# One scan-and-convolution kernel: B times x over the whole array, B turned on TensorE, and a new order of all operations

## The chip, the cores and the metric

The kernel runs on one core of a Trainium2 chip. Its time is device microseconds of one execution; several are taken and the median counts. A profile of one more execution, with its own time and span, tells what each engine did.

## What is computed

Two sequence mixers over S = 2048 positions and D = 640 channels, side by side in one output of 1280 columns. Part A is a diagonal complex state space with 640 states; part B is a four-tap convolution, a gate, and a convolution as long as the sequence.

```python
# part A                                     # part B
B_bar = ((Lam_bar - 1) / Lam)[:, None] * B   k_shift = sum_j k[t - j] * shift_k[:, j]      # 4 taps
Bu    = einsum("bld,pd->blp", x, B_bar)      kv      = k_shift * v
h_t   = Lam_bar * h_{t-1} + Bu_t             y       = causal_conv(kv, ssm_k) + kv * ssm_D # by FFT
y     = 2 * Re(h @ C^T) + x * Dskip          out_B   = q * y
```

## The kernel before, in words

All of it lives in one SBUF tile, `arena`, and one PSUM tile, `acc`, of eight banks of 512 columns. A state's real part stands in partitions 0 to 63 and its imaginary part in 64 to 127, 64 states to a block, ten blocks `j`.

Part A. `load_B` (L482) brings B's real and imaginary rows: the first 256 as plain rows, which TensorE turns against an identity (`turn_B`, L501) and `ev_B` (L503) empties from PSUM, the last 384 by two DMA transposes (L489). `load_x` (L519) brings x by eight DMA transposes, `ld_x0` to `ld_x7`, 256 positions each. `up2`, `up1` and `up0` (L564, L582, L601) form B times x, accumulating over five slices of the 640 channels (`base`, L555), and gather pairs, fours and eights of positions with small rotations `RR` (`rmm`, L577); `ev_up...` empties each result into the tile `A`. A block `up2` is 20 matmuls of up to 512 columns in two banks. Then a scan over coarse positions (`coarse`, `cs_...`), the way back down (`down`: `dn`, and the additions `ad`), and the product with C (`project`: `C`, `ev_C`, with x times Dskip, `xd`, added).

Part B. Four taps (`cm`, products, L198 and L199; `ca`, sums, L799; `cx`, the gate, L800) make kv, which goes to DRAM (`pl`) and comes back in another layout (`rl`). The long convolution is a transform in two steps (`s1`, emptied by `e1`, L845; `s2`, emptied by `e2`, L872) of the filter h and of kv, their product (`pp`, `pq`, `py`, `pz`, L883 to L890), and the way back (`r2`, `r1`). `s1h` needs h, with `ssm_D` added by `addD0` (L768) on GpSimd, and a table `f1` (L274).

The tables are made on the chip, of whole numbers and a sine: GpSimd makes phases (`w_q` L291, `g_q` L330, `phs` L449, `phc` L452, each over 1024 or 1280 columns of int32), ScalarE takes their sine (`w_s`, `g_s`, `sin`, `cos`). The parameters of part A go through a chain of small operations, on VectorE up to `fi` (L378), on GpSimd from `fn1` (L386) to `ph` (L390), on ScalarE `al_s` (L394), on VectorE `al` (L396); four instructions `rr` (L436, 128 x 1280) spread the result to `RR`, which `up1` and `up0` multiply by.

The order is written out by hand: `ORDER` (L1060) lists every operation by number, with its engine (T TensorE, V VectorE, A ScalarE, G GpSimd, S the SyncE queue) and the first of its PSUM banks. Each engine works through its own operations in that order. `emit` (L122) adds the waits: for what an operation reads or overwrites, and, at the first operation of a group, for the last user of its banks. An operation that waits holds up everything behind it on its engine. `warm` (L505) are matmuls of zeros.

What the change and the steps below touch: `load_B`, `BT` (L469), `base`, `rmm` and `ORDER`. In them, `base` issues for each slice d two matmuls of 64 columns, one to each half of the array:

```python
for d in range(5):
    for r in range(2):
        e.matmul(o[64 * r:64 * r + 64], lhsT=self.BT[j][:, r, d, :], rhs=self.XP[:, d, lo:lo + n], start=(d == 0),
                 stop=(d == 4), skip_group_check=True, tile_position=(0, 64 * r))
```

Of the kernel before, what the change touches and what calls it, by code (L numbers as in the profile page):

```python
# [12 lines left out]
bf16 = mybir.dt.bfloat16  # L13
# [447 lines left out]
def mmc(n, par=1):  # L461
    return n * 0.000422 / par


class PartA:
    def __init__(self, c):
        self.c = c
        v = c.v
        self.A = v("A").rearrange("p (j g x) -> p j g x", j=10, g=8)  # L469
        self.BT = []  # L470
        for n, lo in ((2, 0), (2, 1280), (6, 2560)):
            blk = v("BT", lo, 640 * n).rearrange("p (r d j m) -> p r d j m", r=2, d=5, j=n)
            self.BT += [blk[:, :, :, j] for j in range(n)]
# [8 lines left out]
    def load_B(self, k):  # L482
        c, P = self.c, self.c.P
        srcs = ((0, c.ins["A_B_re"]), (1, c.ins["A_B_im"]))
        if k == 2:
            for ri, src in srcs:
                dst = c.v("BT", 2560 + 1920 * ri, 1920).rearrange("p (d m) -> p d m", d=5)
                s = src[256:640, :].rearrange("p (d q) -> p d q", q=128)
                P.add(f"ld_B{k}", {PSP: 1.4}, lambda e, dst=dst, s=s: e.dma_start_transpose(out=dst, in_=s), outs=[dst], nbytes=384 * 1280)  # L489
            return  # L490
        raw, idn = c.v("T", 1280 + 1280 * k, 1280), c.I3[:, 0:128]
# [4 lines left out]
        for r in range(2):  # L496
            g, out, part = P.group(1), c.v("BT", 1280 * k + 640 * r, 640), raw[:, 640 * r:640 * r + 640]
# [5 lines left out]
            P.add("ev_B", {PDVE: .5, PACT: .7}, lambda e, B, out=out: c.CP[e](out=out, in_=B.bitcast(bf16)[:, 0:640]), outs=[out], group=g)  # L503
# [51 lines left out]
    def base(self, e, o, j, lo, n):  # L555
        for d in range(5):
            for r in range(2):
                e.matmul(o[64 * r:64 * r + 64], lhsT=self.BT[j][:, r, d, :], rhs=self.XP[:, d, lo:lo + n], start=(d == 0),  # L558
                         stop=(d == 4), skip_group_check=True, tile_position=(0, 64 * r))
# [4 lines left out]
    def up2(self, j0, q, parts):  # L564
# [3 lines left out]
        for lo, n in parts:  # L568
# [3 lines left out]
            P.add(f"up2{q}_{j0}", {PPE: 10 * .108 * n}, mm, ins=self.base_in(j0, 4 + 2 * q + lo, n) + [self.BT[j0 + 1]], group=g, nmm=20)  # L572
# [4 lines left out]
    def rmm(self, e, o, n, j, x):  # L577
        for r in range(2):
            e.matmul(o[64 * r:64 * r + 64], lhsT=self.c.RR[:, n, j, 64 * r:64 * r + 64], rhs=x, start=False,
                     stop=True, skip_group_check=True, tile_position=(0, 64 * r))  # L580

    def up1(self, j0):  # L582
# [13 lines left out]
        P.add(f"up1_{j0}", {PPE: 12 * .216}, mm, ins=ins, group=g, nmm=24)  # L596
# [359 lines left out]
def build(c):  # L956
# [9 lines left out]
    for k in range(3):  # L966
        a.load_B(k)
# [202 lines left out]
```

## Time and profile before

| what | value |
|---|---|
| median of 3 runs | 198.95 us (196.23 to 199.26) |
| the profiled execution | 199.76 us, span 197.9 us |
| busy: TensorE, VectorE, ScalarE, GpSimd | 178.1, 173.3, 134.0, 76.5 us |
| mean granted TensorE clock | 0.975 |
| moved by DMA | 30.19 MB, 153 GB/s |
| base matmuls of 64 columns (L558) | 440, busy 46.8 us |

The span runs from the first to the last instruction of the profiled execution. Rows of the order of time read: start, length, engine, line, operation, what is written and read, count, and in brackets the idle time before it with what ended it. A matmul's own length holds its fill and its wait in the pipeline, so the pace of matmuls is read from the length of a group on the chain, not from one of them.

### The profile page before, as it was taken

The numbers are of one execution on the slowest core, as the hardware profiler recorded it, in microseconds if no ns is written. First come the engines' busy times: TensorE is split into PE (matmuls) and PEld (weight loads), VectorE is DVE, ScalarE is ACT, GpSimd is POOL, SyncE is SP. The second block draws the span as 40 slices with busy tenths as digits, with TensorE's granted clock in tenths as the row PEclk, the third lists the DMA queues.
The fourth block names the chain that finished last, engine by engine and source line by source line (L and its number), as shares of the span: only waits on it lengthen the run. The fifth ranks groups of instructions, "written<-read, shape, count | busy, mean of one in ns | idle before, by whom it ended". The sixth has DMA issues, their size and how long they took to land.

```text
span 197.9 us, 7928 instructions
## 1 busy us (share of the span) xinstructions
PE 178.1 (90%) x3546; PEld 119.9 (61%) x3549; DVE 173.3 (88%) x230; ACT 134.0 (68%) x160; POOL 76.5 (39%) x63
## 2 busy tenths in 40 slices
PE   5699999779999999788978999999999999999970
PEld 1386555345567765556656666567677867887750
DVE  3969998999789899999999999999999999858650
ACT  2076999845998798999969799796377640870000
POOL 6869972940020400341704465840220604605000
PEclk9799999969999999999999999999999999999996
DMA  6999999599599999899993899002599805433995
GB/s 140 224 206 160 170 170 146 125 183 176 121 231 213 174 179 124 134 193 137 149 251 80 223 165 192 8 3 68 114 211 213 168 14 155 111 85 83 233 208 160
DMA packets 106685, 30.19 MB, mean 153 GB/s; under 512 B 101275, under 2 KB 106011, under 8 KB 106651
## 3 DMA queue, kind: packets, MB, share of 16 engines
q1 hardware_dynamic: 106158, 29.18, 81.0%
q8 instruction: 28, 0.46, 1.1%
q10 hardware_dynamic: 492, 0.50, 1.0%
q14 instruction: 7, 0.05, 0.1%
HBM read 11.32 MB, written 7.86 MB: 97 GB/s over the span
## 4 chain that ended last, share of the span: by engine, by line
PE 41%; DVE 20%; POOL 16%; DMA 9%; issue 7%; ACT 5%; DVEq 0%; ACTq 0%; POOLq 0%
PE acc L718 17%; PE acc L558 8%; POOL arena L291 5%; POOL arena L799 4%; PE acc L904 4%; ACT arena L872 4%; PE acc L859 3%; DMA arena<-in_B_ssm_D_dram 3%; PE acc L840 3%; POOL arena L330 3%; PE acc L925 2%; DMA kv_rows<-arena 2%; DMA arena<-in_A_Lambda_re_dram 2%; DVE arena L872 2%; DVE arena L198 2%
## 5 line engine op out<-in xcount | busy, mean ns | idle before, releaser
L558 PE MATMUL acc<-arena 128*64 128x512 bf16 (+1 forms) x440 | 46.8, 369 | 0.1
L718 PE MATMUL acc<-arena 128*128 128x320 bf16 x320 | 45.7, 300 | 0.6 <-DVE arena L720 0.4
L872 ACT CAST arena<-acc 128x960 bf16<-128x960 f32 (+1 forms) x38 | 33.3, 910 | 9.2 <-PE acc L859 7.4
L718 PEld LDWEIGHTS <-arena 128*128 128x128 bf16 x320 | 30.4, 98 | 13.3 <-DVE arena L720 1.0
L558 PEld LDWEIGHTS <-arena 128*64 128x64 bf16 x440 | 24.6, 113 | 18.7 <-issue 2.4
L845 ACT CAST arena<-acc 128x1024 bf16<-128x1024 f32 x32 | 31.1, 1024 | 7.0 <-PE acc L840 6.6
L909 ACT CAST arena<-acc 128x1024 bf16<-128x1024 f32 x18 | 17.4, 1026 | 9.9 <-PE acc L904 9.8
L859 PE MATMUL acc<-arena 128*64 128x160 bf16 x512 | 21.8, 235 | 1.4 <-ACT arena L845 0.4
L859 PEld LDWEIGHTS <-arena 128*64 128x64 bf16 x512 | 18.1, 110 | 6.4 <-ACT arena L872 1.7
L710 POOL TENSOR_TENSOR arena<-arena 128x640 bf16<-128x640 bf16 x9 | 12.3, 1399 | 15.9 <-DVE arena L888 9.3
L799 DVE TENSOR_TENSOR arena<-arena 128x2048 bf16<-128x2048 bf16 x13 | 18.2, 1401 | 0.3
L720 DVE TENSOR_TENSOR arena<-acc,arena 128x640 bf16<-128x640 f32 x16 | 13.1, 823 | 5.8 <-PE acc L718 4.8
L799 POOL TENSOR_TENSOR arena<-arena 128x2048 bf16<-128x2048 bf16 x2 | 8.3, 4154 | 22.5 <-DVE arena L198 22.5
L886 POOL TENSOR_TENSOR arena<-arena 128x1280 bf16<-128x1280 bf16 x4 | 10.6, 2656 | 16.2 <-DVE arena L883 10.7
L701 DVE TENSOR_TENSOR arena<-acc,arena 128x1024 bf16<-128x1024 f32 (+1 forms) x14 | 16.1, 1169 | 0.3 <-PE acc L682 0.2
L888 POOL TENSOR_TENSOR arena<-arena 128x1280 bf16<-128x1280 bf16 x3 | 8.3, 2772 | 20.0 <-DVE arena L886 19.9
L840 PE MATMUL acc<-arena 64*64 64x64 bf16 x960 | 11.8, 195 | 4.4 <-POOL arena L330 2.5
L840 PEld LDWEIGHTS <-arena 64*64 64x64 bf16 x960 | 9.6, 108 | 9.9 <-issue 4.1
L937 DVE TENSOR_TENSOR arena<-acc,arena 128x960 bf16<-128x960 f32 (+1 forms) x12 | 12.1, 1041 | 2.1 <-PE acc L925 2.1
L198 DVE TENSOR_SCALAR arena<-arena 128x2048 bf16<-128x2048 bf16 (+2 forms) x19 | 12.6, 674 | 1.1 <-issue 0.5
L682 PE MATMUL acc<-arena 128*128 128x512 bf16 (+2 forms) x50 | 12.3, 328 | 0.5 <-ACT arena L845 0.5
L883 DVE TENSOR_TENSOR arena<-arena 128x2560 bf16<-128x2560 bf16 x8 | 12.0, 1504 | 0.2
(142 smaller groups left out, 289.3 us busy)
## 6 DMA issues: line engine op xcount, KB each, us to landing
out_dram<-arena SPq DMA_DIRECT2D x32, 160.0 KB, 3.5
arena<-in_B_ssm_k_dram SPq DMA_DIRECT2D x8, 320.0 KB, 6.4
kv_rows<-arena SPq DMA_DIRECT2D x5, 512.0 KB, 3.5
arena<-kv_rows SPq DMA_DIRECT2D x16, 160.0 KB, 4.4
arena<-in_A_x_dram SPq DMA_DIRECT2D x16, 160.0 KB, 3.6
arena<-in_B_q_dram SPq DMA_DIRECT2D x8, 320.0 KB, 5.7
arena<-in_A_B_im_dram ACTq DMA_DIRECT2D x2, 160.0 KB, 4.1
arena<-in_A_B_re_dram ACTq DMA_DIRECT2D x1, 160.0 KB
```

Source lines behind the costliest of these rows:

```text
L198: vm = lambda e: lambda out, in_, by: e.tensor_scalar_mul(out=out, in0=in_, scalar1=by)
L558: e.matmul(o[64 * r:64 * r + 64], lhsT=self.BT[j][:, r, d, :], rhs=self.XP[:, d, lo:lo + n], start=(d == 0), stop=(d == 4), skip_group_che ...
L682: e.matmul(B[:, o], lhsT=c.RR[:, n, j, :], rhs=fr(j, q, k), start=not by_pe, stop=True, skip_group_check=True)
L701: e.tensor_tensor(out=o, in0=b, in1=o, op=ALU.add)
L718: e.matmul(B[:, 512 * b:512 * b + 320], lhsT=lh[j], rhs=self.CT[:, j, 320 * b:320 * b + 320], start=(j == 0), stop=(j == 9))
L720: P.add(f"ev_C{i}", {PDVE: dve(640)}, lambda e, B: e.tensor_tensor(out=ys.rearrange("p (b n) -> p b n", b=2), in0=B.rearrange("p (b n) -> ...
L799: P.add(f"ca{d}_{j}", tt, lambda e: e.tensor_tensor(out=t1, in0=t1, in1=t2, op=ALU.add), outs=[t1], ins=[t1, t2])
L840: e.matmul(B[64 * b:64 * b + 64, 512 * l + 64 * i:512 * l + 64 * i + 64], lhsT=lh[i][ps], rhs=F[ps, b, 64 * l:64 * l + 64], start=True, st ...
L845: P.add(f"e1{what}{hf}_{u}", {PACT: act(1024), PDVE: dve(1024)}, lambda e, B: c.CP[e](out=out, in_=(B.rearrange("p (l n s k) -> p k s l n" ...
L859: e.matmul(B[64 * s:64 * s + 64, 512 * b + 160 * i:512 * b + 160 * i + 160], lhsT=c.W[:, k, 64 * b:64 * b + 64], rhs=self.AS[hf][:, k, 160 ...
L872: c.CP[e](out=out, in_=b.rearrange("p r (k j n) -> p r k j n", k=n, j=4) if nj > 1 else b.rearrange("p r (k x) -> p r k x", k=n))
L909: P.add(f"er2{hf}_{u}", {PACT: act(1024), PDVE: dve(1024)}, lambda e, B: c.CP[e](out=out, in_=B.rearrange("p (s n b) -> p b s n", s=2, n=4 ...
```

## The change

`base` and `rmm` issue one matmul of 128 columns in place of two of 64, so the weights of a block stand together: `BT` is laid out by 128 rows, five equal pieces, instead of three pieces of different shape. All 640 rows of B now come as plain rows, ten loads of 160 KB, and TensorE turns each (ten `turn_B`, ten `ev_B`, where there were four); the two DMA transposes of B are gone. `ORDER` is new from end to end.

```diff
-        if k == 2:
-            for ri, src in srcs:
-                dst = c.v("BT", 2560 + 1920 * ri, 1920).rearrange("p (d m) -> p d m", d=5)
-                s = src[256:640, :].rearrange("p (d q) -> p d q", q=128)
-                P.add(f"ld_B{k}", {PSP: 1.4}, lambda e, dst=dst, s=s: e.dma_start_transpose(out=dst, in_=s), outs=[dst], nbytes=384 * 1280)
-            return
-        raw, idn = c.v("T", 1280 + 1280 * k, 1280), c.I3[:, 0:128]
+        raw, idn = c.v("T", 1280 + 1280 * k, 1280) if k < 2 else c.v("Y", 1280 * k, 1280), c.I3[:, 0:128]
...
-            g, out, part = P.group(1), c.v("BT", 1280 * k + 640 * r, 640), raw[:, 640 * r:640 * r + 640]
+            g, part = P.group(1), raw[:, 640 * r:640 * r + 640]
+            out = c.v("BT", 1280 * k, 1280).rearrange("p (d j r m) -> p d j r m", d=5, j=2, r=2)[:, :, :, r]
...
     def base(self, e, o, j, lo, n):
         for d in range(5):
-            for r in range(2):
-                e.matmul(o[64 * r:64 * r + 64], lhsT=self.BT[j][:, r, d, :], rhs=self.XP[:, d, lo:lo + n], start=(d == 0),
-                         stop=(d == 4), skip_group_check=True, tile_position=(0, 64 * r))
+            e.matmul(o, lhsT=self.BT[j][:, d, :], rhs=self.XP[:, d, lo:lo + n], start=(d == 0), stop=(d == 4), skip_group_check=True)
...
     def rmm(self, e, o, n, j, x):
-        for r in range(2):
-            e.matmul(o[64 * r:64 * r + 64], lhsT=self.c.RR[:, n, j, 64 * r:64 * r + 64], rhs=x, start=False,
-                     stop=True, skip_group_check=True, tile_position=(0, 64 * r))
+        e.matmul(o, lhsT=self.c.RR[:, n, j, :], rhs=x, start=False, stop=True, skip_group_check=True)
...
-    for k in range(3):
+    for k in range(5):
         a.load_B(k)
...
 ORDER = (
-    "152A0 50G0 140S0 109V0 0V0 75V0 145G0 98G0 6T0 26G0 141G0 153A0 77S0 38G0 146S0 147A0 41G0 168S0 78A0 22G0 13G0 8G0 14V0 "
+    "159A0 41G0 0V0 75V0 6T0 76S0 153A0 8G0 77S0 26G0 13G0 134G0 78A0 15V0 100G0 170S0 50G0 2T1 19V0 7G0 33V0 164A0 16V0 135G0 "
...
```

Lines behind `load_B` shift by five to nine in the changed file: L575 becomes L568, L599 L590, L799 L790, L840 L831, L558 L552.

First place: the SyncE queue at the start, with the semaphores that each transfer waits for (there are eight, taken in turn, so a transfer waits until the one eight before it has landed). Before:

```order
L749 DMA arena<-in_B_shift_k_dram 128x5x4
L348 DMA arena<-in_A_Lambda_im_dram 10x2x64 [waits DVE_49]
L494 DMA arena<-in_A_B_re_dram 128x640
L524 DMA_TRANSPOSE arena<-in_A_x_dram 128x5x256
L489 DMA_TRANSPOSE arena<-in_A_B_im_dram 128x5x384 [waits DMAHW1_49]
L524 DMA_TRANSPOSE arena<-in_A_x_dram 128x5x256 [waits DMAHW2_49]
L489 DMA_TRANSPOSE arena<-in_A_B_re_dram 128x5x384 [waits DMAHW3_49]
L773 DMA_TRANSPOSE arena<-in_B_k_dram 128x2048 [waits DMAHW4_49]
L524 DMA_TRANSPOSE arena<-in_A_x_dram 128x5x256 [waits DMAHW5_49]
```

Now (`ld_x7` is the first of L519, `ld_x6` the second, `ld_x4` the third; five more loads of B stand on ScalarE's queue):

```order
L348 DMA arena<-in_A_Lambda_re_dram 10x2x64 [waits DVE_49]
L348 DMA arena<-in_A_Lambda_im_dram 10x2x64
L488 DMA arena<-in_A_B_re_dram 128x640
L488 DMA arena<-in_A_B_im_dram 128x640
L488 DMA arena<-in_A_B_re_dram 128x640 [waits DMAHW1_49]
L488 DMA arena<-in_A_B_im_dram 128x640 [waits DMAHW3_49]
L519 DMA_TRANSPOSE arena<-in_A_x_dram 128x5x256 [waits DMAHW4_49]
L519 DMA_TRANSPOSE arena<-in_A_x_dram 128x5x256 [waits DMAHW5_49]
L488 DMA arena<-in_A_B_im_dram 128x640 [waits DMAHW6_49]
L519 DMA_TRANSPOSE arena<-in_A_x_dram 128x5x256 [waits DMAHW7_49]
L740 DMA arena<-in_B_shift_k_dram 128x5x4 [waits DMAHW0_49]
L519 DMA_TRANSPOSE arena<-in_A_x_dram 128x5x256 [waits DMAHW1_49]
```

The first x stood behind one load of B on this queue and now stands behind four; k has moved behind x5 and the first piece of h.

Second place: VectorE ahead of the eviction of `up1_0` (L599, now L590). Before, from `ca0_1` to `ca0_0`; `al` (L396) and two `rr` stand further up, ahead of `ev_up20_2`:

```order
L799 TENSOR_TENSOR arena<-arena 128x2048
L416 TENSOR_TENSOR arena<-arena 128x20 [waits DVE_49]
L436 TENSOR_TENSOR arena<-arena 128x1280
L198 TENSOR_SCALAR arena<-arena 128x2048 [waits DVE_49]
L436 TENSOR_TENSOR arena<-arena 128x1280
L575 CAST arena<-acc 128x2x2x256 [waits PE_49,Activation_49]
L599 CAST arena<-acc 128x2x2x256 [waits PE_49]
L799 TENSOR_TENSOR arena<-arena 128x2048 [waits DVE_49]
```

Now, from `al`, right behind `ev_up20_0`, to `ca0_1`; `ev_up1_0` (L590) and `ev_up20_2` (L568) are the next two:

```order
L396 TENSOR_TENSOR arena<-arena 128x80 [waits Activation_49]
L436 TENSOR_TENSOR arena<-arena 128x1280 [waits DVE_49]
L402 MEMSET arena 64x1
L436 TENSOR_TENSOR arena<-arena 128x1280
L274 TENSOR_TENSOR arena<-arena 128x256 [waits Activation_49]
L402 MEMSET arena 64x1
L436 TENSOR_TENSOR arena<-arena 128x1280
L790 TENSOR_TENSOR arena<-arena 128x2048 [waits DMAHW2_49,Activation_49]
L568 CAST arena<-acc 128x2x2x256 [waits PE_49]
L198 TENSOR_SCALAR arena<-arena 128x2048 [waits DMAHW3_49,DVE_49,Pool_49]
L402 MEMSET arena 64x1
L790 TENSOR_TENSOR arena<-arena 128x2048 [waits DVE_49]
```

`al` has moved behind the eviction of `up20_0`, three `rr` follow it at once, and the fourth has gone to GpSimd, behind `addD0`.

Third place: TensorE ahead of the first `s1h` (L840, now L831). Before, behind `up1_4`:

```order
L579 LDWEIGHTS arena
L579 MATMUL acc<-arena 64x512
L840 LDWEIGHTS arena [waits DMAHW1_49,DMAHW3_49,DMAHW0_49,DMAHW4_49,DVE_49,Pool_49]
L840 MATMUL acc<-arena 64x64
L840 LDWEIGHTS arena
```

Now, behind `up21_8`:

```order
L552 LDWEIGHTS arena
L552 MATMUL acc<-arena 128x512
L511 LDWEIGHTS arena [waits DVE_49]
L511 MATMUL acc<-arena 128x512
L511 LDWEIGHTS arena
L511 MATMUL acc<-arena 128x512
L831 LDWEIGHTS arena [waits DMAHW2_49,DMAHW0_49,DMAHW6_49,DVE_49,Pool_49]
L831 MATMUL acc<-arena 64x64
```

`up1_4` has moved behind the first three `s1h`, and `warm0` (L511) stands ahead of them. `warm0` and `s1h0_9` use the bank of `up1_0`, `s1h0_1` that of `up20_2`; VectorE empties both.

More of the change, by code (lines that the diff above doesn't have):

```diff
@@ L595, in up1 @@
             ins += self.base_in(j, 2, 2) + [self.A[:, j, 4:6, 0:256], c.RR[:, 0, j, :]]
[L596 removed]
+        P.add(f"up1_{j0}", {PPE: 12 * .216}, mm, ins=ins, group=g, nmm=12)
         out = self.A[:, j0:j0 + 2, 2:4, 0:256]
@@ L965, in build @@
     b.load_small()
-    for k in range(3):
+    for k in range(5):
         a.load_B(k)
```

11 lines of the change are left out of this document (5 added, 6 removed), and 75 rows, old and new, of the table ORDER.

## Prediction

> **What bounds the kernel now.** I read the page's first part, then the stretches of ten microseconds, then the order of time on each engine up to 45 us, because the new table moves most there.
>
> ```profile
> span 197.9 us, 7928 instructions
> PE 178.1 (90%) x3546; PEld 119.9 (61%) x3549; DVE 173.3 (88%) x230; ACT 134.0 (68%) x160; POOL 76.5 (39%) x63
> PEclk9799999969999999999999999999999999999996
> GB/s 140 224 206 160 170 170 146 125 183 176 121 231 213 174 179 124 134 193 137 149 251 80 223 165 192 8 3 68 114 211 213 168 14 155 111 85 83 233 208 160
> ```
> Two engines are nearly full, TensorE and VectorE. The stretches (busy time of PE, PEld, DVE, ACT, POOL, then clock, DMA share, GB/s) show where each has room:
>
> ```profile
> 20.00:30.00 10.00, 10.00 (x96) 5.29 (x94) 9.72 (x5) 9.82 (x10) 8.56 (x6) 1.00 1.42 170
> 30.00:40.00 10.00, 8.27 (x78) 4.11 (x74) 9.68 (x12) 9.07 (x9) 6.42 (x3) 1.00 0.86 137
> 40.00:50.00 10.00, 9.22 (x214) 4.99 (x216) 9.82 (x12) 5.59 (x5) 2.02 (x2) 0.83 0.89 171
> 60.00:80.00 20.00, 19.24 (x341) 13.83 (x340) 18.92 (x27) 16.70 (x27) 2.53 (x1) 1.00 0.92 174
> 80.00:90.00 10.00, 7.92 (x287) 5.46 (x282) 9.77 (x12) 9.72 (x13) 4.24 (x1) 1.00 1.06 165
> 90.00:100.00 10.00, 9.55 (x168) 6.50 (x159) 9.49 (x12) 9.97 (x14) 4.06 (x1) 1.00 1.20 135
> 100.00:110.00 10.00, 7.75 (x290) 5.97 (x288) 9.80 (x12) 8.07 (x10) 2.70 (x1) 1.00 0.69 190
> 110.00:120.00 10.00, 9.24 (x139) 5.72 (x136) 9.83 (x11) 8.56 (x11) 6.52 (x3) 1.00 0.97 174
> 130.00:160.00 30.00, 29.90 (x507) 22.39 (x494) 28.88 (x32) 21.26 (x25) 6.81 (x3) 1.00 0.67 128
> 160.00:192.00 32.00, 31.24 (x817) 24.02 (x815) 24.50 (x29) 8.29 (x9) 8.24 (x6) 1.00 0.52 131
> ```
> From 20 to 120 us VectorE is the one without gaps. TensorE idles 6.3 us between 60 and 120 (0.76 + 2.08 + 0.45 + 2.25 + 0.76). From 120 on TensorE is full and sets the end. So a delay on VectorE before 120 costs its full length, and one on TensorE alone can be taken up by those 6.3 us. The other loss of TensorE is early:
>
> ```profile
> 2.18 1.52 SPq L524 DMA_TRANSPOSE arena<-in_A_x_dram  x1
> 10.98 24.27 PE L558 MATMUL acc<-arena 128*64 128x256 bf16 x260
> 37.67 0.60 PE L579 MATMUL acc<-arena 128*64 128x512 bf16 x4
> 40.78 0.76 PE L840 MATMUL acc<-arena 64*64 64x64 bf16 x64 [2.51 <-POOL arena L330]
> 18.34 3.17 DVE L436 TENSOR_TENSOR arena<-arena 128x1280 bf16<-128x1280 bf16 x1
> 21.43 3.18 DVE L436 TENSOR_TENSOR arena<-arena 128x1280 bf16<-128x1280 bf16 x1
> 32.86 1.48 DVE L436 TENSOR_TENSOR arena<-arena 128x1280 bf16<-128x1280 bf16 x1
> 35.24 3.17 DVE L436 TENSOR_TENSOR arena<-arena 128x1280 bf16<-128x1280 bf16 x1
> 14.36 2.01 DVE L396 TENSOR_TENSOR arena<-arena 128x80 f32<-128x80 f32 x1 [1.68 <-ACT arena L394]
> 39.47 1.21 DVE L599 CAST arena<-acc 128x1024 bf16<-128x1024 f32 x1
> 16.23 3.93 POOL L291 TENSOR_TENSOR arena<-arena 128x1024 int32<-128x1024 int32 x2
> 23.22 3.14 POOL L291 TENSOR_TENSOR arena<-arena 128x1024 int32<-128x1024 int32 x1
> 11.43 0.19 POOL L386 COPY arena<-arena 128x10 int32<-128x10 int32 x1 [1.71 <-DVE arena L378]
> 33.58 1.20 POOL L768 TENSOR_TENSOR arena<-arena 128x80 bf16<-128x80 bf16 x1 [4.94 <-DMA arena<-in_B_ssm_D_dram]
> ```
> TensorE streams B times x without a break from 10.98, then stands still until 40.78. The profile names GpSimd's L330, but what ends at 40.68 is VectorE's 39.47 + 1.21, `ev_up1_0`: it empties the bank that `s1h0_0` writes, so that is the wait. It costs 2.5 us, and then 1.7 us more, since the clock is granted at 0.83 over the ten microseconds from 40 ((1 - 0.83) x 10).
>
> Why is `ev_up1_0` so late? The same instruction `rr` (L436) takes 3.17 us three times and 1.48 once. 32.86 lies in GpSimd's pause between 28.6 and 33.6. The one at 18.34 ends at 21.51, 1.35 after GpSimd's pair from 16.23 ends at 20.16; and GpSimd's from 23.22, which began inside the second `rr` (it ends at 24.61), takes 3.14 instead of half of 3.93. So operations of the two engines that read and write only SBUF take turns here, each waiting for the other's instruction. Evictions from PSUM (1.21) don't.
>
> **The change, part by part.** Streaming: a pair of 64-column matmuls already runs at the pace of one full one.
>
> ```profile
> 49.55 2.28 PE acc L558 x20
> 51.83 0.43 PE acc L579 x4
> 125.61 0.66 PE acc L682 x3
> 175.44 2.82 PE acc L718 x20
> 183.63 8.27 PE acc L718 x60
> ```
> Ten pairs of 512 take 2.28 us on the chain, two pairs (L579) 0.43, three full matmuls (L682) 0.66: 0.215 to 0.228 for a pair, 0.22 for one. Half the instructions buy no streaming time: 0, bounded by 220 x 0.008 = 1.8 us of gain. Against it, TensorE changes the shape of its tiles 93 times in the new table where it was 88. A change is bounded by the last rows: 20 matmuls alone 2.82, in a run of 60 8.27/3 = 2.76, so 0.06; with ten pairs at 2.28 against 5 x 0.43 = 2.15, 0.13. Five more cost 0.3 to 0.6; I take 0.5. This is what the Trainium skill, TensorEngine Tiling, section Key Properties, warns of: a change of tiling mode drains the engine. Rows and page agree; the page gives no time, and without it the term stays.
>
> The turns of B: 30 more transposes and six more evictions.
>
> ```profile
> L501 PE MATMUL acc<-arena 128*128 128x128 bf16 x20 | 2.2, 265 | 2.4 <-DMA arena<-in_A_B_re_dram 2.4
> L503 DVE COPY arena<-acc 128x640 bf16<-128x640 bf16 x2 | 1.0, 479 | 0.0
> 0.00:10.00 10.00, 5.91 (x28) 2.49 (x29) 6.09 (x33) 1.49 (x2) 7.80 (x23) 0.86 0.90 182
> 10.00:20.00 10.00, 9.90 (x130) 7.09 (x129) 8.07 (x23) 7.05 (x13) 8.40 (x11) 0.97 1.06 181
> ```
> 30 x 0.11 = 3.3 us of TensorE and 6 x 0.48 = 2.9 of VectorE. Both fall ahead of the first product, where TensorE waits for x anyway (4.1 idle before 10) and VectorE has 3.9 + 1.9 idle before 20. One turn of five is left inside the stream: 0.55. Without that cover they would cost 3.3.
>
> The loads: two DMA transposes of 480 KB go, six plain loads of 160 KB come. Nine raw loads now stand ahead of the first x (four did), so x7 is complete after 9 x 0.164 + 0.328 = 1.80 MB. By the page's GB/s, in slices of 4.95 us, 0.69, 1.80, 2.82, 3.61 MB have moved by 4.95, 9.9, 14.8 and 19.8 us. Before, x7 made 0.98 MB, so 6.2 by this count; it landed at about 7.5 (2.18 + 5.3).
>
> ```profile
> DMA to landing us min/median/max: 4.3/5.3/5.4
> ```
> With that 1.3: x7 at 11.2, x6 (2.13 MB) 12.8, x4 15.2, x5 (2.95) 16.9. Before, TensorE started on B times x at 10.98; now at about 11.7, when B's last turn is emptied. Between 10.5 and 13.
>
> Then step by step. A block of 20 instructions cost 24.27/11 = 2.2 us (nine full blocks and four halves). Half a block 11.7 to 12.8, `up21_4` to 15.0, a turn and three halves to 18.8, `up20_0` to 21.0. Four blocks to 29.8, `up1_0` (2.28 + 0.43) to 32.5, two blocks to 36.9. Next in TensorE's queue is `warm0`, which wants the bank of `up1_0`, and `s1h0_1`, which wants that of `up20_2`; everything else on TensorE is queued behind them.
>
> VectorE empties these two at the end of a row of eleven: `ev_up20_0`, `al`, `rr`, `rr`, `f1`, `rr`, `ca0_2`, `ev_up20_4`, `cm0_1`, `ca0_1`, `ev_up1_0`. It can't begin before 21.0, since `al` now stands behind `ev_up20_0` (L396 ran at 14.4). Own time: evictions 3 x 1.21, three `rr` at 1.4, `al` and `f1` 0.55, two `ca` and a `cm` 3.2: 11.6. If nothing interferes `ev_up1_0` ends at 32.6, ahead of need. But GpSimd has, in the same stretch, most of its tables still to make: `fn1` waits for `fi`, now behind eight evictions of B at about 14.7 (11.4 before), and behind it stand `phs`, `phc`, three L291, four L330, `addD0` and one `rr` taken over from VectorE. By turns, each of the seven SBUF steps of VectorE from `al` on waits for a GpSimd step of about 1.95 (the pair above, halved), except where an eviction runs meanwhile: 5 to 6 waits, 10 to 11.5 us. `ev_up1_0` ends between 42.6 and 44.1; if `addD0` (last piece of h, 5.8 MB, so 34 by the same count) is a few us late and GpSimd stands still, near 40.5. I take **43**, against 40.68.
>
> So VectorE is 2.3 us late there. TensorE resumes 1.2 later, at 44.2 instead of 40.78, with `up1_4` (2.7) not yet done: 6.1 late. The half clock after such a stop is paid in both.
>
> Behind that point VectorE's work is as before. By the tables, from `ev_up1_0` on:
>
> ```profile
> L845 DVE CAST arena<-acc 128x1024 bf16<-128x1024 f32 x8 | 9.7, 1220 | 1.4 <-PE acc L840 1.4
> L890 DVE TENSOR_TENSOR arena<-arena 128x1280 bf16<-128x1280 bf16 x8 | 7.4, 926 | 0.1
> ```
> four more evictions of `up` and one more `cm` (4.8 + 0.8) against one fewer L845, `ad`, `cx` and `ev_gC` each (1.2, 1.2, 1.2, 0.8), two fewer small evictions (1.1) and two fewer L890 (1.9) with three more `xd` (1.5): +0. The lag of 2.3 therefore stays until 120. TensorE's 6.1 shrinks in its idle time of 6.3, but not below VectorE's 2.3, since that idle time is largely a wait for VectorE: I leave 0.7 of it. Sum: 2.3 + 0.7 + 0.5 = **+3.5 us**. The profiled execution took 199.76 us (span 197.9), 0.8 over the median of 198.95; 199.76 + 3.5 = 203.3, and on the median's scale **202.5 us**, slower by 1.8%.
>
> **The rivals.** *Taking turns costs less than this* (the other side: faster). If GpSimd is held up by `addD0` or its tables fall outside the stretch, `ev_up1_0` ends near 33, TensorE runs through at 36.9 with 2.7 less done than at 40.78, and no half clock: 1.2 + 1.7 earlier, and VectorE's lead lets a little more of the 6.3 go: 4.5, so 194.5. It decides once `ev_up1_0` ends before 36.9. For it: `rr` at 1.48; against: only a GpSimd pause made that.
>
> *The lag is absorbed*: GpSimd also takes a `cx` and two L890 from VectorE behind 60 us, and if VectorE catches up its 2.3 us there, only the 0.5 is left: 199.5. For it, TensorE's 6.3 us of idle; against, that VectorE's sum is no smaller.
>
> *Worse*: TensorE's 6.1 isn't absorbed at all, because the same VectorE that is late feeds it: 198.95 + 6.1 + 0.5 = 205.5. To it belongs a slow start. In the second slice of the page's clock row (7 tenths) the clock is down behind a stretch that held ten transposes and a pause; nine turns now fill the time ahead of the stream, and if they don't raise the clock, its first 3.4 us run at half (as around 40, where 1.7 lost is 3.4 at half): 1.7 more. The Trainium skill, TensorE: Matmul & The Clock Gate, Part 4, says so: transposes don't count as work for the clock gate. No row here separates that.
>
> **How the numbers follow.** Forecast 0.42, turns cost less 0.20, absorbed 0.20, worse 0.18. A measurement here tells about 2% from no change, that is 195.0 to 202.9. Faster: three quarters of the second case, 0.15. Slower: the fourth and nearly half of the first, 0.38. Same: 0.47. Range 195 to 207: it leaves out most of the second case's half below 195 and a tail above; the forecast's own range is 200.5 to 205.
>
> **What would show it.** Right: TensorE idle from about 37 to 43 with `ev_up1_0` at its end, L436 on VectorE again near 3.2 us, `al` behind 21, first base matmul 10.5 to 13, 20 full matmuls of 512 in 4.3 to 4.6 us. Wrong: no stop of TensorE before `s1h0_1`; L436 at 1.4; full matmuls clearly faster than 0.215; or a new, longer wait on x or h.

## The result, and the profile after

| | before | changed |
|---|---|---|
| median | 198.91 us (196.23 to 199.26, 4 executions) | 208.35 us (206.66 to 210.72, 4 executions) |
| the profiled execution | 199.76 us, span 197.9 us | 208.58 us, span 206.8 us |

The ratio is 1.049, with a 95% interval of 1.034 to 1.065: slower, the way the sum was forecast (the chances had given "same" more than "slower"), but by more than twice the forecast 1.8%, and outside the range of 195 to 207. (A ratio compares only executions within 1.5% of the fastest of their kernel; where a kernel's executions lie further apart than that, their range is given with it.)

The page of the changed kernel: span, busy time, and the clock granted to TensorE in 40 slices of 5.2 us.

```profile
span 206.8 us, 7444 instructions
PE 184.2 (89%) x3296; PEld 120.0 (58%) x3296; DVE 175.7 (85%) x236; ACT 137.7 (67%) x163; POOL 87.1 (42%) x62
PEclk9999996999999999995799999999999999889999
```

Before, between the lower slices at its start and its end, the row of the clock had one dip, near 41 us. Now it has three: the 6, the 57 and the 88. The stretches of ten microseconds (busy time of PE, PEld, DVE, ACT, POOL, then clock, DMA share, GB/s) show which of them comes with a stop:

```profile
30.00:40.00 10.00, 8.75 (x32) 3.49 (x32) 9.97 (x7) 2.31 (x3) 9.91 (x5) 0.83 0.78 129
90.00:100.00 10.00, 6.42 (x143) 4.57 (x139) 8.33 (x5) 4.64 (x7) 3.73 (x1) 0.68 0.88 99
170.00:180.00 10.00, 8.23 (x180) 6.45 (x179) 7.77 (x10) 2.84 (x3) 5.11 (x3) 0.95 0.33 86
```

The middle one is new: TensorE busy for 6.42 us where it was 9.55, clock 0.68 where it was 1.00, VectorE issues 5 instructions where there were 12. The table of TensorE's waits (engine, line, what it waited for, us) names the three longest:

```profile
PE acc L673 <- DVE arena L653: 3.6, 1, 3.6
PE acc L552 <- ACT arena L568: 3.2, 1, 3.2
PE acc L916 <- issue: 1.7, 1, 1.7
```

L653 is `cs_h1`, a step of the coarse scan, 128 x 640 on VectorE (L662 before). The order of time on VectorE, then GpSimd, then TensorE around it:

```profile
89.10 0.82 DVE L547 CAST arena<-acc 128x640 bf16<-128x640 f32 x1
89.84 4.64 DVE L653 TENSOR_TENSOR arena<-arena 128x640 bf16<-128x640 bf16 x1
94.38 2.00 DVE L692 TENSOR_TENSOR arena<-acc,arena 128x1024 bf16<-128x1024 f32 x2
```

```profile
85.35 4.25 POOL L790 TENSOR_TENSOR arena<-arena 128x2048 bf16<-128x2048 bf16 x1 [13.88 <-DVE arena L198]
89.68 4.05 POOL L791 TENSOR_TENSOR arena<-arena 128x2048 bf16<-128x2048 bf16 x1
```

```profile
90.60 0.45 PE L831 MATMUL acc<-arena 64*64 64x64 bf16 x32
94.63 0.69 PE L673 MATMUL acc<-arena 128*128 128x128 bf16 x5 [3.58 <-DVE arena L653]
```

Before the change the same instruction, then L662, took 0.90 us:

```profile
86.44 0.90 DVE L662 TENSOR_TENSOR arena<-arena 128x640 bf16<-128x640 bf16 x1
```

GpSimd's L791 is `cx3`, which the new table gives to GpSimd instead of VectorE. It begins at 89.68, 0.16 us ahead of `cs_h1`, and ends at 93.73; `cs_h1` ends at 94.48, 0.75 later, a little less than its own length of 0.9. So it waited for all that was left of `cx3`. TensorE, which wants `cs_h1` for the next `dn`, stood for 3.58 us, and then ran at half clock. The three windows of half clock, each as a stretch of its own:

```profile
32.13:35.54 3.41, 3.41 (x10) 1.21 (x9) 3.41 (x3) 0.00 (x0) 3.32 (x3) 0.50 1.08 210
93.57:100.40 6.83, 5.77 (x111) 4.11 (x111) 5.03 (x6) 2.72 (x3) 0.16 (x1) 0.50 0.97 97
178.90:182.32 3.42, 3.42 (x77) 3.36 (x69) 2.05 (x2) 1.54 (x2) 0.96 (x1) 0.50 0.32 101
```

Half of what TensorE works in each is lost: 1.7, 2.9 and 1.7 us. The last of the three follows the stop in L916. Before, after the first product, one such window (41.3 to 44.7) cost 1.7. All of the difference can be put into four sums, worked out from the trace of each profiled execution, from the first matmul of B times x to the last matmul of all:

| us | before | changed | difference |
|---|---|---|---|
| B times x begins | 10.98 | 10.05 | -0.93 |
| TensorE without work | 9.71 | 14.71 | +5.00 |
| half of its work at half clock | 1.71 | 6.30 | +4.59 |
| the rest: matmuls at their pace | 169.49 | 170.86 | +1.37 |
| last matmul ends | 191.89 | 201.93 | +10.04 |

What follows the last matmul is 1.1 shorter, so the span grows by 8.9. Stops and clock make it, in about equal shares; the matmuls themselves add little.

### The profile page after: what moved, and what is told of

Its sections match the earlier page's. It is cut to its first block, busy times and chain, and to the rows that moved or that the text cites. A ratio compares the mean times of both kernels' runs of the same rounds, so it can differ in the third digit from the quotient of the medians.

```text
span 206.8 us, 7444 instructions
## 1 busy us (share of the span) xinstructions
PE 184.2 (89%) x3296; PEld 120.0 (58%) x3296; DVE 175.7 (85%) x236; ACT 137.7 (67%) x163; POOL 87.1 (42%) x62
## 4 chain that ended last, share of the span: by engine, by line
PE 62%; ACT 15%; DVE 10%; issue 5%; DMA 3%; SPq 1%; ACTq 0%; DVEq 0%
PE acc L709 18%; PE acc L552 15%; PE acc L850 7%; PE acc L895 5%; PE acc L571 4%; ACT arena L863 4%; PE acc L673 4%; PE acc L831 3%; ACT arena L836 3%; DMA arena<-in_A_x_dram 2%; ACT arena L568 2%; DVE arena L653 2%; PE acc L672 2%; ACT arena L900 1%; PE acc L826 1%
## 5 line engine op out<-in xcount | busy, mean ns | idle before, releaser
L552 PE MATMUL acc<-arena 128*128 128x512 bf16 (+1 forms) x220 | 46.7, 367 | 3.2 <-ACT arena L568 3.2
L709 PEld LDWEIGHTS <-arena 128*128 128x128 bf16 x320 | 30.3, 98 | 14.0 <-DVE arena L711 1.1
L836 ACT CAST arena<-acc 128x1024 bf16<-128x1024 f32 x33 | 32.2, 1029 | 6.8 <-PE acc L826 4.0
L552 PEld LDWEIGHTS <-arena 128*128 128x128 bf16 x220 | 21.1, 99 | 24.3 <-ACT arena L568 3.7
L900 ACT CAST arena<-acc 128x1024 bf16<-128x1024 f32 x18 | 17.2, 1023 | 11.8 <-PE acc L895 11.8
L850 PEld LDWEIGHTS <-arena 128*64 128x64 bf16 x512 | 17.8, 110 | 5.6 <-issue 1.7
L790 DVE TENSOR_TENSOR arena<-arena 128x2048 bf16<-128x2048 bf16 x13 | 19.1, 1469 | 0.2
L790 POOL TENSOR_TENSOR arena<-arena 128x2048 bf16<-128x2048 bf16 x2 | 8.3, 4157 | 22.1 <-DVE arena L198 22.1
L877 POOL TENSOR_TENSOR arena<-arena 128x1280 bf16<-128x1280 bf16 x4 | 10.5, 2615 | 16.8 <-DVE arena L874 16.8
L673 PE MATMUL acc<-arena 128*128 128x512 bf16 (+2 forms) x50 | 13.4, 352 | 3.7 <-DVE arena L653 3.6
L692 DVE TENSOR_TENSOR arena<-acc,arena 128x1024 bf16<-128x1024 f32 (+2 forms) x13 | 13.7, 1069 | 2.0 <-PE acc L673 1.9
L831 PEld LDWEIGHTS <-arena 64*64 64x64 bf16 x960 | 10.0, 111 | 6.3 <-ACT arena L836 2.3
L199 ACT ACTIVATE arena<-arena 128x2048 bf16<-128x2048 bf16 x4 | 8.0, 1999 | 7.7 <-DVE arena L790 7.7
L831 PE MATMUL acc<-arena 64*64 64x64 bf16 x960 | 12.0, 198 | 1.1 <-POOL arena L330 0.6
L571 PE MATMUL acc<-arena 128*128 128x256 bf16 (+2 forms) x70 | 12.0, 298 | 1.0 <-DVE arena L612 0.9
L895 PE MATMUL acc<-arena 64*128 64x128 bf16 x320 | 12.3, 240 | 0.1
```

Source lines behind the costliest of these rows:

```text
L552: e.matmul(o, lhsT=self.BT[j][:, d, :], rhs=self.XP[:, d, lo:lo + n], start=(d == 0), stop=(d == 4), skip_group_check=True)
L571: e.matmul(o, lhsT=self.c.RR[:, n, j, :], rhs=x, start=False, stop=True, skip_group_check=True)
L673: e.matmul(B[:, o], lhsT=c.RR[:, n, j, :], rhs=fr(j, q, k), start=not by_pe, stop=True, skip_group_check=True)
L692: e.tensor_tensor(out=o, in0=b, in1=o, op=ALU.add)
L709: e.matmul(B[:, 512 * b:512 * b + 320], lhsT=lh[j], rhs=self.CT[:, j, 320 * b:320 * b + 320], start=(j == 0), stop=(j == 9))
L790: P.add(f"ca{d}_{j}", tt, lambda e: e.tensor_tensor(out=t1, in0=t1, in1=t2, op=ALU.add), outs=[t1], ins=[t1, t2])
```

## The experiments

In the tables' tokens below, 456 is `cx3`, 338 `cs_h1`, 287 the eviction `ev_gC2_1`, 130 to 132 are `rr` (130 is the one that `up1` multiplies by); a letter is the engine. In the kernel before, 440 is `cx3`, 322 `cs_h1`, 328 `ad2_0`.

**`cx3` back on VectorE.**

```diff
-456G0 344V4
+344V4 456V0
```

> The changed kernel with one letter of the table back: cx3 (L791) on VectorE again, behind ad2_0, as before the change it was on VectorE. Theory (cx3 on GpSimd holds cs_h1 for its whole length, 4.7 us instead of 0.9, and the stop of TensorE behind it is followed by 6.8 us at half clock): 3.8 + 3.4 us go, 1.2 us of cx3 come back to VectorE, so 201 to 203 us, cs_h1 near 0.9, and no half clock between 93 and 100. Rival (VectorE is full, so its work counts and not who does it; cx3 back on VectorE gives its 1.2 us back and the stop is only moved): 206 us or more, and the half clock stays in that stage.

Measured: 204.95 us (204.43 to 205.94), ratio 1.036 (1.026 to 1.046). `cs_h1` took its own length again:

```profile
90.50 0.89 DVE L653 TENSOR_TENSOR arena<-arena 128x640 bf16<-128x640 bf16 x1
```

The stop ahead of L673 and the half clock behind it are gone, and from 34.7 us to the last matmul the clock was whole. The median fell by 3.4 us; the theory's range of 201 to 203 was missed by 2. The profiled execution doesn't isolate the collision. By the sums above, time without work fell from 14.71 to 12.87 and what the clock took from 6.30 to 1.55, 6.6 us together; but of that, 1.7 and 1.7 belong to the stop in L916 and its half clock, which didn't come in this execution. Against it, stops of 0.7 to 1.0 us that weren't there stand at 93.8, 106.2 and 129.5, B times x began at 11.02 instead of 10.05, behind a half clock from 7.3 to 10.8, and the matmuls took 1.5 longer. The last matmul ends 4.1 earlier. The mechanism is right; the price of the collision in the total is smaller than its 6.5 us in place.

**The `rr` for `up1_0` first.**

```diff
-131V0
+130V0
...
-130V0
+131V0
```

> The changed kernel with two equal instructions rr (L436) on VectorE exchanged, so that the part of RR that up1_0 multiplies by is made first of the three and not last. TensorE's stop from 27.8 to 31.05 should go in any case. Theory (VectorE's row up to ev_up1_0 sets this stage, TensorE's stop costs nothing of its own): TensorE then stops ahead of warm0 until ev_up1_0 at 40.8 instead, and the time is 207 to 208.5 us. Rival (the stop of 3.2 us and the 1.7 us lost at half clock behind it are on the path): 203 to 205 us.

Measured: 208.47 us (206.91 to 212.02), ratio 1.047 (1.031 to 1.064): no gain, as the theory said. The stop moved, whole and a little longer, to the next instruction that wants something of VectorE (before the exchange it stood at 31.05 for 3.23 and at 40.88 for 1.08):

```profile
40.68 1.03 PE L511 MATMUL acc<-arena 128*128 128x512 bf16 x2 [5.62 <-DVE arena L590]
```

It also corrects a name: the profile put the stop at 31.05 down to ScalarE's L568, which ended at 30.9; the third `rr` ended at 30.95, and the exchange of two `rr` removed the stop.

**Pairs of 64 columns again**, in the changed kernel with its order.

```diff
-            e.matmul(o, lhsT=self.BT[j][:, d, :], rhs=self.XP[:, d, lo:lo + n], start=(d == 0), stop=(d == 4), skip_group_check=True)
+            for r in range(2):
+                e.matmul(o[64 * r:64 * r + 64], lhsT=self.BT[j][:, d, 64 * r:64 * r + 64], rhs=self.XP[:, d, lo:lo + n], start=(d == 0),
+                         stop=(d == 4), skip_group_check=True, tile_position=(0, 64 * r))
```

> The changed kernel with its own order and its own B, but base and rmm (L552, L571) again as pairs of 64-column matmuls, one to each half of the array. Theory (a pair runs at the pace of one full matmul; full columns buy nothing and cost some tile changes at most): 207.5 to 208.5 us. Rival (full columns are faster, by the 1.8 us that was the bound, and the loss elsewhere hides it): 209.5 to 210.5 us.

Measured: 201.9 us (200.97 to 203.41), ratio 1.020 (1.009 to 1.032): 6.5 us less, which neither theory allowed. The trace shows where, on VectorE and on GpSimd (L657 is `cs_h1`, L795 `cx3`):

```profile
90.15 0.89 DVE L657 TENSOR_TENSOR arena<-arena 128x640 bf16<-128x640 bf16 x1
```

```profile
85.86 4.25 POOL L794 TENSOR_TENSOR arena<-arena 128x2048 bf16<-128x2048 bf16 x1 [13.93 <-DVE arena L198]
90.19 4.75 POOL L795 TENSOR_TENSOR arena<-arena 128x2048 bf16<-128x2048 bf16 x1
```

The pairs moved both engines by some tenths. `cs_h1` now began 0.04 us ahead of `cx3`, took 0.89, and it was `cx3` that waited (4.75 instead of 4.05). So the largest loss hangs on who is first, by a tenth of a microsecond. Not all of the 6.5 us is the race: the half clock behind the stop late in the kernel (1.7) didn't come here either, and the last runs below find pairs 0.6 to 1.4 faster than full columns.

**The new code in the old order**: the kernel before's table, with the ten loads, turns and evictions of B; six of the ten turns lie inside the stream of B times x, two each ahead of `up21_2`, `up21_4` and `up21_6`.

> The changed kernel's code (B times x over 128 columns, all 640 rows of B turned on TensorE) with the order of the kernel before; only the six plain loads of B, the six turns and the six evictions that the old table didn't have are put in: loads behind x7, x6 and ahead of x4, two turns each ahead of up21_2, up21_4 and up21_6, evictions half on ScalarE and half on VectorE. Theory (the new order lost the time, the new code costs or gains under 2 us): 197.5 to 201 us. Rival (the code loses it: more raw loads ahead of x, turns inside the stream, evictions in strided pieces): 203 us or more.

Measured: 203.12 us (201.12 to 204.97), ratio 1.018 (1.002 to 1.033): the median just reaches the rival's 203, the ratio stands for 202.4, between rival and theory. So the new code, with six turns in the stream, loses part of the time by itself. The two matmul groups around a pair of turns stand 0.56 us apart, so the six cost 1.7 where the new table hides all but one of ten. The remaining 2 us of this kernel I can't place.

**`cs_h1` ahead of the eviction**, `cx3` left on GpSimd.

```diff
+338V0
 287V4
...
-338V0
```

> The changed kernel with one exchange in VectorE's row: cs_h1 (L653) goes ahead of the eviction ev_gC2_1, and so begins at about 89.1 us, 0.6 ahead of GpSimd's cx3 at 89.7, which stays where it is. Theory (of two operations that only touch SBUF the one that comes first runs alone and the other waits; the loss is decided by who comes first): cs_h1 takes 0.9 us, cx3 waits instead, no stop of TensorE and no half clock between 90 and 100, 200 to 203 us. Rival (cx3 on GpSimd is too slow for what follows it, or the stage is short of VectorE time whoever comes first): 206 us or more.

Measured: 205.35 us (204.05 to 206.19), ratio 1.024 (1.016 to 1.031). `cs_h1` came while `ca3_0` still ran, waited for its end (1.18 us in all) and was first; `cx3` waited (4.56).

```profile
88.09 1.18 DVE L653 TENSOR_TENSOR arena<-arena 128x640 bf16<-128x640 bf16 x1
```

```profile
84.27 4.25 POOL L790 TENSOR_TENSOR arena<-arena 128x2048 bf16<-128x2048 bf16 x1 [13.88 <-DVE arena L198]
88.60 4.56 POOL L791 TENSOR_TENSOR arena<-arena 128x2048 bf16<-128x2048 bf16 x1
```

The stage from 90 to 100 was whole: 9.79 busy, clock 1.00. The theory's 203 us at most are missed by 2.4. The stop in L916 (172.9, 1.32 us, with a half clock from 175.1 to 178.5 behind it) doesn't explain that, since the changed kernel has it too. By the sums, the clock took 2.9 less, but time without work fell only from 14.71 to 13.99: the stop of 3.6 us is gone, and the other stops together are 2.9 longer. The last matmul ends 3.6 earlier, the median is 3.0 lower.

**The same with pairs.** The one change is that of the run with pairs above.

> The kernel of the run before this one, with base and rmm again as pairs of 64-column matmuls: the two differ by nothing but the matmuls. Theory (streaming is the same, the pairs' 6.5 us in the earlier run came from cs_h1 by chance beginning 0.1 us ahead of cx3): within 0.5 us of the kernel with full columns. Rival (pairs are faster in themselves, by the clock or by the loading of weights): 3 us or more below it. Other rival (full columns are faster, by up to the bound of 1.8): 1 to 1.8 us above it.

Measured: 204.14 us (201.21 to 207.88), ratio 1.019 (1.013 to 1.024). Not usable for the matmuls, but a good picture of the race. In the profiled execution `cs_h1` arrived 0.26 us behind `cx3` and paid for it, although it stood one eviction earlier:

```profile
88.59 4.53 DVE L657 TENSOR_TENSOR arena<-arena 128x640 bf16<-128x640 bf16 x1
```

```profile
88.33 4.05 POOL L795 TENSOR_TENSOR arena<-arena 128x2048 bf16<-128x2048 bf16 x1
```

**The kernel before with `cx3` on GpSimd**, and nothing else.

```diff
-440V0
+440G0
```

> The kernel before the change, with cx3 alone moved to GpSimd. There cs_h1 begins at 86.4 and GpSimd's ca3_0 ends at 86.5, so cs_h1 should come first. Theory (who comes first decides): no block, cs_h1 0.9 us, 197.5 to 200 us. Rival (cx3 on GpSimd costs as such, by its 4 us length or by holding back cm4 and ca4): 202 us or more.

Measured: 198.21 us (197.82 to 201.54), ratio 0.988 (0.981 to 0.996). No block: `cs_h1` at 84.8, 0.9 us long, and `cx3` at 86.6, held up by the load of v, not by `ca3_0`; the two didn't meet. So `cx3` on GpSimd costs this kernel nothing as such. This is the fastest version here; I don't call the 1.2% a gain of the move, since in the profiled execution it is the half clock behind the stop at 38.5 (2.31 us) that didn't come, 1.7 us.

**The same with `cs_h1` one step later.**

```diff
-322V0
 329T4
 328V6
+322V0
```

> The kernel before the change, with cx3 moved to GpSimd and cs_h1 behind ad2_0 (1.2 us) instead of ahead of it: cs_h1 now comes at 87.6, about a microsecond behind the start of cx3 at 86.6. Theory: cs_h1 waits for cx3 to end near 90.8 and ends at 91.7 (length near 4 us instead of 0.9), TensorE stops and the clock falls behind it: 203 to 206 us. Rival (cx3 on GpSimd and VectorE's SBUF work run side by side, and the long cs_h1 of the changed kernel had another cause): within 1.5 us of the kernel before, 198 to 200.5 us, cs_h1 near 0.9 to 1.5.

Measured: 202.64 us (198.55 to 209.52), by the median between theory and rival; ratio 1.003 (0.997 to 1.009). Inconclusive as a test, since the load of v brought `cx3` later than I had reckoned; the two began together, `cs_h1` at 88.12 (0.88 us long) and `cx3` at 88.11 (4.78):

```profile
88.12 0.88 DVE L662 TENSOR_TENSOR arena<-arena 128x640 bf16<-128x640 bf16 x1
```

```profile
88.11 4.78 POOL L800 TENSOR_TENSOR arena<-arena 128x2048 bf16<-128x2048 bf16 x1 [1.69 <-DMA arena<-in_B_v_dram]
```

One kernel with 11 us between its executions is what a dead heat would give. That the long ones are those in which `cx3` won is argued, not shown: only one execution was profiled.

**A base for the rest**: `cs_h1` ahead of the eviction, and `cm3_0` (454) behind `cs_b1`, so that `ca3_0` ends later.

```diff
-454V0
 340A2 337V0
+454V0
```

> The changed kernel with cs_h1 ahead of ev_gC2_1 as in the earlier run, and cm3_0 behind cs_b1, so that GpSimd's ca3_0 and cx3 come half a microsecond later and cs_h1 is already waiting when ca3_0 ends. It is the base of the three that follow. Theory (who comes first decides): cs_h1 near 1 us, no half clock between 90 and 100, 201 to 205 us; the upper end if TensorE again stops for 1.3 to 1.7 us without a wait between 172 and 179 and is halved behind it. Rival (the stage is short of VectorE time, so the loss returns elsewhere): 206 us or more.

Measured: 204.31 us (201.65 to 207.42), ratio 1.021 (1.014 to 1.029). `cs_h1` 1.54 us with its wait for `ca3_0`, clock whole from 46.7 to the last matmul.

**The base with pairs.**

> The base kernel of this call with base and rmm as pairs of 64-column matmuls and nothing else. Theory (the same pace): within 1 us of the base kernel, L552's stretch of 220 full matmuls as long as the 440 halves. Rival (full columns cost something in themselves): 2 us or more below the base; other rival (they gain): 1 us or more above it.

Measured: 203.76 us (201.04 to 206.75), ratio 1.016 (1.008 to 1.024). Its profiled execution again lost the race (`cs_h1` 4.52 us), the base's had won it: not usable either.

**VectorE's row in another order.** The two `rr` for `up0` go behind `ev_up1_6` (257), and `ev_up1_0` (233) and `ev_up20_2` (213) go ahead of `cm0_1` (386). Part of the edit:

```diff
+212T6 233V4 213V6 386V0
 229A2
-212T6 386V0
...
 257V2
+131V0 132V0
```

> The base kernel of this call with VectorE's row ahead of the first s1h in another order: of the three rr only the one that up1_0 needs stays there, the two that up0 needs go behind ev_up1_6, and the evictions of up1_0 and up20_2 go ahead of cm0_1 and ca0_1. VectorE's work is the same. TensorE's stops between 27 and 42 us (3.2, 1.3 and 0.6 us) and the half clock there (1.7 us) should be gone or under 1.5 us in all. Theory of the prediction (VectorE's work sets the end until 120, so TensorE's earlier start is given back): 0 to 2 us below the base. Rival (TensorE's stops and its clock count, VectorE has room behind them): 4.5 to 6.5 us below the base, so 196 to 199 us.

Measured: 205.94 us (203.35 to 206.67), ratio 1.030 (1.022 to 1.038): no gain, 1.6 us above the base's median. The stop moved on again, to the bank that ScalarE's `ev_up21_8` empties; that stood behind `cm0_0`, which waited for VectorE's `ca0_1`:

```profile
41.56 4.45 PE L552 MATMUL acc<-arena 128*128 128x512 bf16 x10 [5.70 <-ACT arena L568]
```

**And two of GpSimd's tables later**, with ScalarE's sine (61) of the first.

```diff
-60G0
...
-64G0
...
-61A0
...
 133G0
+60G0 64G0
...
+61A0
```

> The kernel before this one, with two tables of GpSimd (g_q, L330, about 2.3 us each) moved out of VectorE's row from 21 to 33 us to behind GpSimd's rr. Theory (operations of the two engines on SBUF take turns): rr, f1, ca0_2 and cm0_1 of VectorE lose 2 to 5 us of waiting in that stretch, and the time falls by 0 to 1.5 us more if TensorE was still waiting there. Rival (the tables cost VectorE nothing, its long instructions have another cause): the lengths of rr and ca0_2 stay at 2.9 us.

Measured: 206.57 us (203.48 to 209.24), ratio 1.030 (1.020 to 1.040). A miss: `rr` and `ca0_2` had already become short (1.5 and 1.8 us) with the new row, and the tables now met `ca0_0` and `cx0` instead, 2.62 and 2.80 us where the kernel without this move had 1.2 each.

**The next waiters too**, in the new row without the moved tables: `ev_up21_8`, `w_s` and `e1h0_9` ahead of `cm0_0` (388) on ScalarE, `e1h0_7` and `ev_up1_6` ahead of `ca0_0` and `cx0` (389, 390) on VectorE.

```diff
-388A0
...
 209A4
+388A0
...
 257V2
+389V0 390V0
```

> The kernel with VectorE's row in another order (the run that only moved TensorE's stop), and now ScalarE's and VectorE's next steps as well: ev_up21_8, the last sine w_s and e1h0_9 go ahead of cm0_0 on ScalarE, e1h0_7 and ev_up1_6 ahead of ca0_0 and cx0 on VectorE. TensorE's stop of 5.7 us from 35.9 to 41.6, which was a wait for ev_up21_8 behind cm0_0 behind ca0_1, should fall to 1.5 us or less, with no half clock there. Theory of the prediction (VectorE's work sets the end until 120, an earlier TensorE gives its lead back): 0 to 2 us below the base with cs_h1 ahead, so 202 to 204.5. Rival (the early stops and the clock behind them count in full): 4.5 to 6.5 us below it, 197.5 to 200.

Measured: 203.19 us (202.63 to 204.33), ratio 1.026 (1.021 to 1.031). TensorE now ran through from 27 to 42 without a stop. It gained 1.1 us on the base's median, and by the ratios nothing. Much of the lead was given back at 53.17, to the eviction of `up1_8`, behind the VectorE work that had been put off:

```profile
53.17 0.45 PE L831 MATMUL acc<-arena 64*64 64x64 bf16 x32 [2.84 <-DVE arena L590]
```

`cs_h0` ended at 80.4, as in the run with `cs_h1` ahead, whose early stops (3.2, 1.3, 0.6) were all there. In the base's own profile it ended at 82.6, with stops of 2.9, 3.0 and 0.6, so against the base part of the lead was kept.

**The same with `cx3` on VectorE**, and then **with pairs** (the edits are those of the first and third run).

> The kernel before this one with cx3 on VectorE, so that nothing of GpSimd can come ahead of cs_h1. Theory (the collision is a matter of who comes first, and is gone in both): within 1.5 us of it, and its executions lie closer together. Rival (cx3 on VectorE costs its own 1.2 us and what queues behind it): 2 us or more above it.

> The kernel before this one with base and rmm as pairs of 64-column matmuls: without a race in the stage the two differ by the matmuls alone. Theory (a pair runs at the pace of one full matmul): within 1 us. Rival (full columns gain, up to the bound of 1.8): 1 to 2 us above. Other rival (full columns lose): 1 us or more below.

Measured: 204.91 us (204.33 to 206.25), ratio 1.035 (1.029 to 1.041), and with pairs 203.50 us (201.28 to 204.11), ratio 1.025 (1.019 to 1.031). Without a race the executions lie within 2 and 3 us. `cx3` on VectorE costs 1.7 us, where its own length is 1.2. Pairs are 1.4 us faster than full columns, the other rival, and the two disturbed comparisons point the same way by 0.6 and 1.2. The traces don't place it: the last matmul ends at the same time (196.6 and 196.9), B times x begins at 9.8 and 11.1, with pairs the stops are 2.6 shorter and the clock takes 2.0 more, and the "rest" is within half a microsecond (171.8 and 171.4).

## Why the prediction was wrong: step by step

**What bounds the kernel, and the turns.** Right, and more right than it was used. Operations that only touch SBUF did take turns: in the stretch that the prediction spoke of, the second `rr`, `f1`, the third `rr`, `ca0_2` and `ca0_1` were drawn out again.

```profile
21.22 1.49 DVE L436 TENSOR_TENSOR arena<-arena 128x1280 bf16<-128x1280 bf16 x1
22.83 2.99 DVE L436 TENSOR_TENSOR arena<-arena 128x1280 bf16<-128x1280 bf16 x1
25.74 2.11 DVE L274 TENSOR_TENSOR arena<-arena 128x256 bf16<-128x256 f32 x1
27.98 2.97 DVE L436 TENSOR_TENSOR arena<-arena 128x1280 bf16<-128x1280 bf16 x1
30.87 2.91 DVE L790 TENSOR_TENSOR arena<-arena 128x2048 bf16<-128x2048 bf16 x1
36.89 2.80 DVE L790 TENSOR_TENSOR arena<-arena 128x2048 bf16<-128x2048 bf16 x1
39.62 1.21 DVE L590 CAST arena<-acc 128x1024 bf16<-128x1024 f32 x1
```

`ev_up1_0` ended at 40.8, not 43: VectorE had begun on the row at 19.3 instead of 21. So the term of 2.3 us in the sum measured 0.15 (40.83 against 40.68).

**The start.** B times x began at 10.05; I had 11.7, and 10.5 as the lower bound. The clock was whole there, so the slow start of the rival "worse" did not come in this execution; in the profile of the first run, whose program is the same up to there, the clock was at half from 7.3 to 10.8.

```profile
10.05 3.42 PE L552 MATMUL acc<-arena 128*128 128x256 bf16 x20
```

**Streaming.** Right in the trace: ten full matmuls of 512 columns take on the chain what ten pairs took (2.28).

```profile
58.74 2.27 PE acc L552 x10
...
61.45 2.16 PE acc L552 x10
```

In the time, full columns cost 1.4 us against pairs, of the sign of my 0.5 for changes of tile shape and nearly three times its size. That tile changes are the cause is not shown.

**The cover of the turns of B.** Right: ahead of the first product they cost nothing; inside the stream six cost 1.7, at 0.28 each, about half of my 0.55.

**TensorE's stop.** Predicted from 37 to 43, with `s1h0_1` at 44.2. It came in two parts, 27.8 to 31.05 for the `rr` and 39.8 to 42.06, with `warm0` inside the second and one half clock between: I had priced three `rr` but not asked which of them `up1_0` reads. The three runs that reordered this stretch show the rest of the reasoning right: each stop taken from TensorE came back later, at a step that waits for VectorE directly or through ScalarE. In time they gained at most 1.1 us.

**"Behind that point VectorE's work is as before: +0."** This is the step that failed. Three marks and the end show the lag against the kernel before: 0.15 us at `ev_up1_0`, 3.1 at the end of `cs_h0` (81.5 against 78.4), 7.1 at the end of `cs_h1` (94.48 against 87.34), 10.0 at the last matmul. So nearly all of it arose behind the point where I had added nothing.

The 3.1 at `cs_h0` equals the 2.3 + 0.7 that I carried there only by luck, since the 2.3 wasn't there. Part of it stands in the page as a wait that the kernel before doesn't have on VectorE, for k, whose second and third transfer the new table issues at 41.8 and 54.0 instead of 35.4 and 50.5. The first row is the kernel before, the second the changed one:

```profile
L198 DVE TENSOR_SCALAR arena<-arena 128x2048 bf16<-128x2048 bf16 (+2 forms) x19 | 12.6, 674 | 1.1 <-issue 0.5
L198 DVE TENSOR_SCALAR arena<-arena 128x2048 bf16<-128x2048 bf16 (+2 forms) x21 | 13.5, 671 | 2.9 <-DMA arena<-in_B_k_dram 2.8
```

That this wait sets the lag is not shown: in the run with the other `rr` first it was 0.3 us, and `cs_h0` ended at 81.7. The cause of these 3 us stays open.

The 4 us at `cs_h1` are shown. I compared VectorE's work as a sum of lengths, and took `cx3` on GpSimd for a relief ("absorbed": GpSimd also takes a `cx` from VectorE). By my own rule it was a new partner to take turns with, 4 us long, next to a step that TensorE waits for. It cost 3.6 us in place, and by the clock another 2.9; the runs with `cx3` elsewhere, or behind `cs_h1`, show both gone. In the total they gain less than these 6.5: 3.4 and 3.0 us in the median, 2.7 and 5.1 by the ratios, since other stops grow. The forecast of 202.5 was too low by 5.9, so the collision is about half of that or more. The rival "worse", nearest in number with 205.5, shares the step: it adds nothing behind `s1h0_1` either. Without the collision the kernel is at 1.02 to 1.04 of before, where the forecast had 1.02.

The Trainium skill, SBUF — State Buffer, Who interferes with whom, states the rule that I should have carried past 43 us: issue order decides which of the two engines is held up, and for the whole instruction. The traces agree: 0.16 us behind cost 3.7 (4.64 against 0.90), 0.26 behind 3.6 (4.53), 0.04 ahead cost nothing. A start within 0.01, in the run with `cs_h1` one step later, cost it nothing either.

**"The half clock after such a stop is paid in both."** Right for that stop and too little: I priced none for later ones, and 4.6 of the 10.0 us are clock, 2.9 behind `cs_h1` and 1.7 behind the stop in L916.

**What no step had** is the stop inside L916 at 177, 1.66 us and 1.7 of clock. No run takes it alone away, so what it adds to the total is not shown.

## What to carry to other kernels

When a table moves a step between VectorE and GpSimd, its price is not its length but its neighbour: look up which SBUF-only instruction of the other engine will be issued within its length, and who waits for that one. Where such a pair arrives within a few tenths of a microsecond, small shifts elsewhere decide who waits: put the short step that others wait for so far ahead that it is already waiting when the long one could start, or give both to one engine. An eviction ahead was enough here with full columns and not with pairs. And price a stop of TensorE with the window of half clock that may follow it, 1.7 us for 3.4, before asking which stop to remove; where another engine sets the pace, removing one mostly moves it.

## What the runs showed of the hardware that I had not expected

**A stop without a wait, at a fixed place in the program.** In eight of the nine profiled kernels with full columns and the new table's order, or one close to it, TensorE stood for 1.3 to 1.7 us in the middle of one `r1` (L916), between two matmuls with nothing to wait for. For example, with `cx3` on VectorE and the new row:

```profile
172.20 0.37 PE L916 MATMUL acc<-arena 64*64 64x80 bf16 x20
173.95 0.30 PE L916 MATMUL acc<-arena 64*64 64x80 bf16 x12 [1.38 <-issue]
```

and in the ninth, the first run, whose TensorE program is the changed kernel's, not at all:

```profile
175.43 0.48 PE L916 MATMUL acc<-arena 64*64 64x80 bf16 x32
```

It is always at the same instruction, about the 5569th of TensorE's in the trace; in the four kernels with pairs at the 7105th, 1536 later, in another group (L713), 1.3 to 1.9 us. The page counts transfers of 16,384 bytes as a queue of kind "instruction", 26 of them here:

```profile
q8 instruction: 26, 0.43, 0.9%
```

With 6630 of TensorE's instructions in the trace that is 255 to a transfer, and 1536 is six times 256, so by the count they carry TensorE's program. In all twelve kernels with the stop one of these transfers ended shortly before TensorE went on: at 177.3 in the changed kernel, 1.4 us before, and 1.3 to 1.7 us before in the others. In the first run the same transfer, the 21st, ended at 171.4, 4.2 us before TensorE came to that instruction, and there was no stop. So the times point to a wait for late instructions; why the transfer is late in the one and not in the other stays open.

**The length of a stop doesn't tell whether the clock falls.** A stop of 1.32 us (172.9) and one of 1.66 (177.1) were followed by a window at half, one of 2.31 (38.5, the kernel before with `cx3` on GpSimd) and another of 1.66 (177.5, the run with `rr` first) were not. Between the first product and the last matmul all windows were 3.41 us or twice that. Of the eight stops in L916, all of 1.3 to 1.7 us, three were followed by such a window. The Trainium skill, TensorE: Matmul & The Clock Gate, Why this matters for your kernels, advises against gaps of more than about 3 us between bursts of matmuls; by these traces shorter ones aren't safe either.
